# A block-sorted attention with a two-branch network behind it on one core: the first stage's steps join the hand-written list, and the list is laid anew

## The chip, the cores and the metric

One core of a Trainium2 chip. The metric is the device time of one execution in microseconds (us); lower is better. The core's engines are TensorE (PE; its weight loads are shown apart as PEld), VectorE (DVE), ScalarE (ACT), GpSimd (POOL) and SyncE (SP). Each works its own queue of instructions in order, and they meet at semaphores. Here POOL issues all loads, which also turn float32 into bf16; SP issues the transposing DMAs and nearly all stores.

## The reference

```python
# q, k, v: (4, 8, 768, 64); sort_net: (4, 8, 8, 8); block = 96
P = sort_net
for _ in range(5):
    P = P - max(P, -1); P = exp(P)
    P = P / (sum(P, -1) + 1e-9)
    P = P / (sum(P, -2) + 1e-9)
k_sorted = einsum('bhij,bhjcd->bhicd', P, k_blocks)      # the same for v
scores = scale * q_blocks @ k_sorted^T                    # block by block
out = softmax(scores) @ v_sorted
x = out as (3072 tokens, 512)
h1, h2 = x @ w1, x @ w2                                   # w1, w2: 512 x 1024
return max(h1, h2) @ w_out                                # w_out: 1024 x 512
```

## The kernel before

The four batches are worked one after another and overlapped by hand. max(h1, h2) is taken as relu(x (w1 - w2)) + x w2: `d` forms w1 - w2 in place, `T` turns w2 on PE and `c` multiplies it with w_out, so that the second part goes into the output product directly. The output product is done in halves by Strassen's scheme with seven products instead of eight: `P` for two of a half's three token tiles, `U` for the third. The h product of the last batch is done in the same way (`Y`).

Almost all of the work is an order written out by hand: a list of short words, `plan`, that `token` turns into calls one by one. All engines' queues follow from that list: a word appends its instructions to the queue of each engine that it uses, so a word's place is its place in every one of them. A letter at a word's end names the engine that does the conversion out of PSUM or the sum: A for ACT, D for DVE, P for POOL. The words:

- `kb.t`: PE sorts a third of k of batch b, one conversion to kT. `bb.t`: the same for v, into v_sb. `tb.n`: turns a quarter of v (two batches at once) within SBUF, which the sort of v needs. `B`: block diagonals of batches 1 to 3.
- `qb.h`: q turned, by PE and a conversion for b = 0 and 1, by two DMA transposes on SP for b = 2 and 3, which need `pb.0` and `pb.1` (copies that pair heads).
- `sb.u`: scores (8 matrix multiplications) and their exp on ACT. `vb.u`: 8 more, then on DVE a reciprocal `rs` and a multiplication `x`. `xb.t`: x turned into xT, on PE for b = 0 and by an SP transpose for the others.
- `ha`, `hb`, `h`: halves or the whole of an h product, `hb` and `h` with the relu. `X`, `G`, `w`, `Z`: sums for Strassen's scheme (xT, g, weights). `P3.4A`: batch 3, step 4, conversion on ACT.
- `lk`, `lq`, `lf`, `lv`: POOL loads of k, q and v. `y`: POOL waits for xT and qT before it overwrites v_dc.

PSUM has four buffers (`bufs=4`). A word that needs one takes a free one and holds it until its conversion has read it; `P` and `U` hold one over seven steps.

Before the list stands the first stage in plain code: loads of v, k and q of batch 0, five Sinkhorn rounds (`sinkhorn`, a chain of small DVE instructions and one exp on ACT each, with fills on PE), `masks`, the turn of v (`turn_v`, in five parts), `block_diagonals_first` and `sort_k(0, 0)`. The weights' loads follow it, behind two small POOL copies into a tile `seen`, one of which reads `p_bf` (the last Sinkhorn round's result) and the other kT: POOL can't go on to the loads before these exist.

```python
    nc.gpsimd.tensor_copy(out=seen[0:G, 0], in_=p_bf[:, NB - 1, NB - 2 :])
    load_w_columns(w2_sb, moe_w2, 0, 1)
...
    sort_k(0, 0, 640, "A")
    nc.gpsimd.tensor_copy(out=seen[:, 1], in_=kT[0][:, 0:2])
    load_w_columns(w1_sb, moe_w1, 0, 1)
```

Of the kernel before, what the change touches and what calls it, by code (L numbers as in the profile page):

```python
# [1221 lines left out]
```

## Time and profile before

| | |
|---|---|
| three runs | 159.38 (median), 159.37, 160.71 us |
| profiled execution, span | 157.9 us; the page gives no other time for it |
| PE busy | 149.7 us (95%) |
| DVE busy | 127.1 us (81%) |
| ACT busy | 84.4 us (53%) |
| POOL busy | 29.3 us (19%) |
| granted PE clock | full in all 40 slices |

The span runs from the first to the last instruction. "Busy" is time in which an engine has an instruction in work; an engine that issues DMAs or waits isn't busy, except that POOL's own DMA issues are instructions of it. The loads that POOL issues land in this order (issue and landing by the trace, us):

| load | issued | landed | | load | issued | landed |
|---|---|---|---|---|---|---|
| v of batch 0, 3 pieces | 1.24 to 2.40 | 5.50, 7.31, 8.57 | | k1 | 19.63 | 36.05 |
| k0, 3 pieces | 3.47 to 4.56 | 9.81, 11.88, 12.66 | | q1 | 24.43 | 40.04 |
| q0, 4 pieces | 5.08 to 7.59 | 13.64, 14.62, 15.63, 16.57 | | v1, v2, 4 pieces | 25.01 to 27.59 | 42.65 to 47.54 |
| w2 and w1, 4 of 256 KB | 11.40, 13.90, 14.64, 15.96 | 18.65, 19.54, 20.93, 22.23 | | q2 | 31.22 | 51.39 |
| w2 and w1, 2 of 512 KB | 16.69, 17.43 | 24.80, 27.30 | | k2 | 32.67 | 55.27 |
| w_out, 2 of 512 KB | 18.16, 18.89 | 29.89, 32.39 | | k3 | 39.94 | 59.29 |

### The profile page before, as it was taken

What the parts mean: (1) busy time and instruction counts of PE and PEld (TensorE: products, weight loads), DVE (VectorE), ACT (ScalarE), POOL (GpSimd) and SP (SyncE); (2) the same over time, 40 slices, a digit from 0 to 9 for tenths busy, and PEclk for the clock granted to TensorE, in tenths of its full rate; (3) what the DMA queues carried; (4) which work ended last, traced back from release to release, by engine and by line L of the source; (5) the groups of instructions that cost most, each with busy time, mean ns of one, the idle gap of its engine ahead of it and who ended that gap; (6) DMA issues with size and microseconds to landing.
All of it is one profiled execution on the core that took longest, in us unless ns stands there. A gap on an engine that the chain in (4) does not pass through costs nothing.

```text
span 157.9 us, 5185 instructions
## 1 busy us (share of the span) xinstructions
PE 149.7 (95%) x2260; PEld 115.1 (73%) x2264; DVE 127.1 (81%) x274; ACT 84.4 (53%) x111; POOL 29.3 (19%) x57
## 2 busy tenths in 40 slices
PE   6989799999999999999999999999999999999980
PEld 6839577756467788887676898766689886578870
DVE  4879799939969998892899989979878959799340
ACT  3489795656159993459148700793662106692010
POOL 7969997220100000004300000000000000000000
PEclk9999999999999999999999999999999999999999
DMA  2999999999999999795999995750020719000063
GB/s 40 192 204 199 186 202 205 214 214 216 213 203 217 214 145 192 261 132 174 143 220 211 138 147 115 238 215 0 4 50 4 111 42 395 0 4 0 18 254 129
DMA packets 28918, 23.93 MB, mean 152 GB/s; under 512 B 16672, under 2 KB 24608, under 8 KB 28896
## 3 DMA queue, kind: packets, MB, share of 16 engines
q0 software_dynamic: 9280, 13.37, 48.3%
q1 hardware_dynamic: 19200, 9.84, 26.0%
q8 instruction: 17, 0.28, 0.7%
q10 hardware_dynamic: 416, 0.39, 0.7%
q14 instruction: 5, 0.04, 0.1%
HBM read 26.75 MB, written 6.29 MB: 209 GB/s over the span
## 4 chain that ended last, share of the span: by engine, by line
PE 80%; DMA 9%; DVE 6%; issue 1%; POOL 0%; ACT 0%; DVEq 0%; POOLq 0%
PE out_ps L934 33%; PE h_ps L711 20%; DMA q_raw<-in_q_dram 6%; PE wc_ps L691 4%; PE o_ps L609 4%; DMA v_raw<-in_v_dram 3%; PE hb_ps L779 3%; DVE x L626 3%; PE s_ps L581 3%; PE hq_ps L779 2%; PE k_ps L486 2%; PE v_ps L551 2%; PE tw_ps L672 1%; PE tq_ps L453 1%; DVE o L960 1%
## 5 line engine op out<-in xcount | busy, mean ns | idle before, releaser
L711 PE MATMUL h_ps<-xT,w_sb 128*128 128x384 bf16 x192 | 33.9, 326 | 0.1
L597 ACT ACTIVATE e<-s_ps 96x768 bf16<-96x768 f32 x32 | 23.8, 808 | 13.3 <-PE s_ps L581 13.1
L711 PEld LDWEIGHTS <-w_sb 128*128 128x128 bf16 x192 | 17.8, 98 | 10.8
L725 ACT ACTIVATE g<-h_ps 128x768 bf16<-128x768 f32 x20 | 16.0, 812 | 15.1 <-PE h_ps L711 14.9
L626 DVE TENSOR_TENSOR x<-o_ps,rs 96x512 bf16<-96x512 f32 x32 | 22.0, 687 | 1.1
L934 PEld LDWEIGHTS <-g 128*128 128x128 bf16 x192 | 18.3, 98 | 2.3
L934 PEld LDWEIGHTS <-sums_g 128*128 128x128 bf16 x144 | 13.7, 98 | 1.7
L960 DVE TENSOR_TENSOR o<-out_ps,a 128x512 f32<-128x512 f32 (+1 forms) x20 | 11.0, 550 | 3.4 <-PE out_ps L934 2.1
L960 DVE TENSOR_TENSOR o<-out_ps,o 128x512 f32<-128x512 f32 (+1 forms) x16 | 8.8, 555 | 5.6 <-PE out_ps L934 5.5
L934 PE MATMUL out_ps<-wo_sb,g 128*128 128x256 bf16 x96 | 13.1, 273 | 0.0
L609 PEld LDWEIGHTS <-e 96*128 96x128 bf16 x256 | 10.8, 98 | 2.4 <-DVE x L626 0.2
L609 PE MATMUL o_ps<-v_sb,e 96*128 96x65 bf16 x256 | 12.1, 193 | 0.1
L934 PE MATMUL out_ps<-w2T,sums_x 128*128 128x256 bf16 x72 | 11.8, 273 | 0.0
L109 ACT CAST v_sb<-v_ps 96x1024 bf16<-96x1024 f32 x10 | 9.7, 1027 | 0.4 <-PE v_ps L528 0.4
L934 PEld LDWEIGHTS <-sums_x 128*128 128x128 bf16 x96 | 9.0, 98 | 1.2
L581 PE MATMUL s_ps<-qT,kT 64*128 64x96 bf16 x256 | 8.9, 204 | 0.7 <-issue 0.4
L620 DVE RECIPROCAL rs<-o_ps 96x8 f32<-96x8 f32 x32 | 6.3, 197 | 3.4 <-PE o_ps L609 3.2
L581 PEld LDWEIGHTS <-kT 64*128 64x128 bf16 x256 | 6.3, 94 | 3.6 <-issue 2.6
L109 ACT CAST kT<-k_ps 128x1024 bf16<-128x1024 f32 x7 | 7.0, 1013 | 3.4 <-PE k_ps L486 3.4
L969 ACT COPY o<-out_ps 128x512 f32<-128x512 f32 (+1 forms) x7 | 3.5, 503 | 9.7 <-PE out_ps L934 9.7
L111 DVE CAST v_sb<-v_ps 96x1024 bf16<-96x1024 f32 x6 | 7.3, 1216 | 1.2 <-PE v_ps L528 0.8
L779 PEld LDWEIGHTS <-w_sb 128*128 128x128 bf16 x56 | 5.5, 98 | 3.5
(135 smaller groups left out, 272.4 us busy)
## 6 DMA issues: line engine op xcount, KB each, us to landing
out_dram<-o SPq DMA_DIRECT2D x10, 512.0 KB, 3.3
v_raw<-in_v_dram POOLq DMA_DIRECT2D x8, 384.0 KB, 15.5
k_raw<-in_k_dram POOLq DMA_DIRECT2D x3, 768.0 KB, 19.3
w_sb<-in_moe_w_dram POOLq DMA_DIRECT2D x4, 256.0 KB, 6.3
w_sb<-in_moe_w_dram POOLq DMA_DIRECT2D x2, 512.0 KB, 9.0
wo_sb<-in_moe_w_out_dram POOLq DMA_DIRECT2D x2, 512.0 KB, 12.6
v_raw<-in_v_dram POOLq DMA_DIRECT2D x3, 256.0 KB, 5.4
k_raw<-in_k_dram POOLq DMA_DIRECT2D x3, 256.0 KB, 7.9
```

The lines of the kernel that those rows point to most:

```text
L109: nc.scalar.copy(out=out_ap, in_=in_ap)
L111: nc.vector.tensor_copy(out=out_ap, in_=in_ap)
L581: nc.tensor.matmul(ps[:, h2 * 512 + ii * 128 : h2 * 512 + ii * 128 + BLK], kT[b][rows, (hp * 8 + i) * BLK : (hp * 8 + i) * BLK + 128], rhs ...
L597: nc.scalar.activation(out=e_out, in_=src, func=AF.Exp, scale=scale)
L609: nc.tensor.matmul(ps[:, h2 * 512 + ii * 65 : h2 * 512 + (ii + 1) * 65], e[:, (h2 * 4 + ii) * BLK : (h2 * 4 + ii) * BLK + 128], v_sb[:, m0 ...
L626: nc.vector.tensor_tensor(out=x, in0=ov[:, :, :, 0:D], in1=rs.to_broadcast([BLK, 2, 4, D]), op=ALU.mult,)
L691: nc.tensor.matmul(ps[:, 0:512], w2T[:, fb, dmt * 128 : (dmt + 1) * 128], wo_sb[:, fb, :], start=(fb == 0), stop=(fb == NFB - 1),)
L711: nc.tensor.matmul(h_ps[ch, t][:, m * 512 : m * 512 + TCH], w1_sb[:, hp, fb * 128 : (fb + 1) * 128], xT[:, b % 2, ch, hp % 2, hp // 2, :], ...
L725: nc.scalar.activation(out=g, in_=src, func=AF.Relu)
L779: nc.tensor.matmul(ps[:, m * 512 : m * 512 + TCH], w[:, k, c : c + 128], x[:, k], start=new and k == 0, stop=k == 1, skip_group_check=True,)
L934: ins = nc.tensor.matmul(self.ps[:, bank * 512 + p * NW : bank * 512 + (p + 1) * NW], left(self.b, lw, k, ti * 128), right(rw, k), start=n ...
L960: ins = nc.vector.tensor_tensor(out=self.part(ch, half), in0=self.by_tile(self.bank(n)), in1=other, op=ALU.add)
```

## The change

The loads of the first stage are split into single DMAs that have words of their own (`lw`, `lk0.p`, `lq0.p`, `a`), and so have the rest of the first stage (`I` identity, `J` first selections, `S` Sinkhorn rounds, `m` masks, `g` selections, `D0` first block diagonals, `tv` turns of v, `f` fills). All steps are in one list, whose order is new throughout. The two copies into `seen` are gone. w2 comes in four column pieces instead of three. The first sort of k loses its fill of 640 columns, and a fill of the same size (`f4`) stands behind the first Sinkhorn round. The tiles that hold exp's results are taken from a list of free ones instead of in rotation. Some conversions change between ACT and DVE. PE's instructions are the same in number (4530 rows of its queue in both). On POOL, lf1 now comes ahead of k1 and q1, and k3 ahead of k2. On SP, the store of P0's first half and x1.2 now come ahead of q2's transposes.

```diff
@@ -132,7 +132,7 @@
 
     QC = S // 16
 
-    def load_q(b):
+    def load_q(b, part=None):
         if b == 1:
             q_raw[b] = qpool.tile([128, QC * D], BF16, tag="q_raw", name="q_raw", bufs=1)
             nc.gpsimd.dma_start(
@@ -143,10 +143,12 @@
             home = w2_sb.rearrange("p t f -> p (t f)") if b == 2 else v_dc
             t = home[:, 0 : H * R * D].rearrange("p (h x) -> p h x", h=H)
         else:
-            t = qpool.tile([128, H, R * D], BF16, tag="q_raw", name="q_raw", bufs=1)
+            if b not in q_raw:
+                q_raw[b] = qpool.tile([128, H, R * D], BF16, tag="q_raw", name="q_raw", bufs=1)
+            t = q_raw[b]
         src = q[b].rearrange("h (p r) d -> p h (r d)", r=R)
-        for hs in [slice(0, H)] if b else [slice(hp, H, HP) for hp in range(HP)]:
-            nc.gpsimd.dma_start(out=t[:, hs], in_=src[:, hs])
+        hs = slice(0, H) if b else slice(part, H, HP)
+        nc.gpsimd.dma_start(out=t[:, hs], in_=src[:, hs])
         q_raw[b] = t
 
     k_raw = {}
@@ -155,10 +157,11 @@
     v_src = v.rearrange("b h (j c) d -> b (h j) (c d)", j=NB)
     NCH = 3
 
-    def load_k(b):
-        k_raw[b] = kpool.tile([128, HB * D], BF16, tag="k_raw", name="k_raw")
+    def load_k(b, part=0):
+        if part == 0:
+            k_raw[b] = kpool.tile([128, HB * D], BF16, tag="k_raw", name="k_raw")
         n = HB * D // (1 if b else NCH)
-        for ci in range(1 if b else NCH):
+        for ci in [part]:
             nc.gpsimd.dma_start(
                 out=k_raw[b][:, ci * n : (ci + 1) * n],
                 in_=k_src[b, :, ci * n : (ci + 1) * n],
@@ -177,24 +180,20 @@
     w2_sb = big.tile([128, HP, DFF], BF16, tag="w2", name="w2_sb")
     wo_sb = big.tile([128, NFB, DMODEL], BF16, tag="wo", name="wo_sb")
 
-    def load_w(dst, src):
+    def load_w(dst, src, i):
         s = src.rearrange("(t p) f -> p t f", p=128)
         n = s.shape[1] // 2
-        for i in range(2):
-            nc.gpsimd.dma_start(
-                out=dst[:, i * n : (i + 1) * n, :], in_=s[:, i * n : (i + 1) * n, :]
-            )
+        nc.gpsimd.dma_start(
+            out=dst[:, i * n : (i + 1) * n, :], in_=s[:, i * n : (i + 1) * n, :]
+        )
 
     def load_w_columns(dst, src, t0, t1):
         s = src.rearrange("(t p) f -> p t f", p=128)
         c = slice(t0 * DFF // 4, t1 * DFF // 4)
         nc.gpsimd.dma_start(out=dst[:, :, c], in_=s[:, :, c])
 
-    load_v(0, 3)
+    load_v(0, 3, which=0)
     ident = const.tile([128, 128], BF16, tag="ident", name="ident")
-    make_identity(nc, ident)
-    load_k(0)
-    load_q(0)
 
     id64 = const.tile([128, 64], FP32, tag="id64", name="id64")
     maskJ = const.tile([128, 7, NB], FP32, tag="maskJ", name="maskJ")
@@ -219,14 +218,16 @@
         )
 
     one_j = const.tile([G, 8 * 130], BF16, tag="one_j", name="one_j")
-    nc.gpsimd.memset(one_j.bitcast(U32), 0)
-    nc.gpsimd.tensor_copy(
-        out=one_j.rearrange("g (j x) -> g j x", x=130)[:, :, 0:128].rearrange(
-            "g j (h w) -> g j h w", w=16
-        )[:, :, :, 0:2],
-        in_=ident[0:G, 0:8].to_broadcast([G, 8, 2, NB]).transpose([0, 3, 1, 2]),
-    )
-    selections(0)
+
+    def first_selections():
+        nc.gpsimd.memset(one_j.bitcast(U32), 0)
+        nc.gpsimd.tensor_copy(
+            out=one_j.rearrange("g (j x) -> g j x", x=130)[:, :, 0:128].rearrange(
+                "g j (h w) -> g j h w", w=16
+            )[:, :, :, 0:2],
+            in_=ident[0:G, 0:8].to_broadcast([G, 8, 2, NB]).transpose([0, 3, 1, 2]),
+        )
+        selections(0)
 
     def w_difference(t, eng=None):
         n = DFF // 4
@@ -562,7 +563,7 @@
             eng=eng,
         )
 
-    e_tiles, x_tiles, e_next = {}, {}, [0]
+    e_tiles, x_tiles, e_free = {}, {}, list(e_bufs)
 
     def scores(b, u, n=0):
         ih, hp = divmod(u, HP)
@@ -585,8 +586,7 @@
                     start=True,
                     stop=True,
                 )
-        e = e_bufs[e_next[0] % NE]
-        e_next[0] += 1
+        e = e_free.pop(0)
         src = ps[0:BLK].rearrange("p (t f) -> p t f", t=8)[:, :, 0:BLK]
         if b == 1:
             e_out = e[:, 0 : 8 * BLK].rearrange("p (t ch c) -> p t ch c", t=8, ch=2)
@@ -601,6 +601,7 @@
     def values(b, u, n=0):
         ih, hp = divmod(u, HP)
         e = e_tiles.pop((b, u))
+        e_free.append(e)
         m0 = (b % 2) * 64
         ps = ps_f32("o_ps")
         keep_streaming(ps, n)
@@ -1053,40 +1054,20 @@
                         in_=self.both,
                     )
 
-    first, second, both = slice(0, 64), slice(64, 128), slice(0, 128)
+    def spread_masks():
+        for c, n, m in [(2, 2, 0), (4, 3, 1)]:
+            nc.gpsimd.tensor_copy(
+                out=maskJ[:, c : c + n],
+                in_=maskJ[:, m].to_broadcast([128, NB, n]).transpose([0, 2, 1]),
+            )
+
+    first = slice(0, 64)
+    weights = {
+        1: (load_w_columns, w1_sb, moe_w1),
+        2: (load_w_columns, w2_sb, moe_w2),
+        3: (load_w, wo_sb, moe_w_out),
+    }
     keep_streaming(ps_f32("fill_ps"), 92 * 118, most=118)
-    for it in range(5):
-        sinkhorn(it)
-        if it < 3:
-            masks(it)
-        if it == 2:
-            turn_v(first, "A", 0, 18)
-        if it == 3:
-            turn_v(first, "A", 18, 36)
-    for c, n, m in [(2, 2, 0), (4, 3, 1)]:
-        nc.gpsimd.tensor_copy(
-            out=maskJ[:, c : c + n],
-            in_=maskJ[:, m].to_broadcast([128, NB, n]).transpose([0, 2, 1]),
-        )
-    turn_v(first, "A", 36, 56)
-    turn_v(first, "A", 56, 80)
-    block_diagonals_first()
-    seen = const.tile([128, 2, 2], BF16, tag="seen", name="seen")
-    nc.gpsimd.tensor_copy(out=seen[0:G, 0], in_=p_bf[:, NB - 1, NB - 2 :])
-    load_w_columns(w2_sb, moe_w2, 0, 1)
-    selections(1)
-    selections(2)
-    turn_v(first, "D", 80, 96)
-
-    sort_k(0, 0, 640, "A")
-    nc.gpsimd.tensor_copy(out=seen[:, 1], in_=kT[0][:, 0:2])
-    load_w_columns(w1_sb, moe_w1, 0, 1)
-    load_w_columns(w2_sb, moe_w2, 1, 2)
-    selections(3)
-    load_w_columns(w1_sb, moe_w1, 1, 2)
-    load_w_columns(w2_sb, moe_w2, 2, 4)
-    load_w_columns(w1_sb, moe_w1, 2, 4)
-    load_w(wo_sb, moe_w_out)
 
     def token(text):
 
@@ -1095,7 +1076,25 @@
         kind = body.rstrip("0123456789.")
         n = [int(x) for x in body[len(kind) :].split(".")]
         engine = {"P": nc.gpsimd, "D": nc.vector}.get(eng)
-        if kind == "k":
+        if kind == "I":
+            make_identity(nc, ident)
+        elif kind == "J":
+            first_selections()
+        elif kind == "S":
+            sinkhorn(n[0])
+        elif kind == "m":
+            masks(n[0]) if n[0] < 3 else spread_masks()
+        elif kind == "g":
+            selections(n[0])
+        elif kind == "D":
+            block_diagonals_first()
+        elif kind == "tv":
+            turn_v(first, eng, *n)
+        elif kind == "f":
+            keep_streaming(ps_f32("fill_ps"), n[0] * 160, most=320)
+        elif kind == "a":
+            weights[n[0]][0](*weights[n[0]][1:], *n[1:])
+        elif kind == "k":
             sort_k(*n, eng=eng)
         elif kind == "q":
             q_transposes(*n, eng)
@@ -1122,9 +1121,11 @@
         elif kind == "lv":
             load_v(3, half=n[0])
         elif kind == "lk":
-            load_k(n[0])
+            load_k(*n)
         elif kind == "lq":
-            load_q(n[0])
+            load_q(*n)
+        elif kind == "lw":
+            load_v(0, 3, which=n[0])
         elif kind == "w":
             weight_sums(*n, engine)
         elif kind == "c":
@@ -1163,29 +1164,30 @@
     landed = const.tile([128, 4], BF16, tag="landed", name="landed")
     plan = [
         """
-        k0.1D k0.2A b0.2A b0.0D b0.3A q0.0D q0.1D s0.4 b0.1D s0.5 s0.6 s0.7 lk1 v0.4 s0.0 v0.6
-        s0.3 v0.5 d0P s0.1 T1D s0.2 d1P v0.7 x0.2A v0.1 T0A x0.3D ha0.1.0 v0.0 ha0.1.1 v0.2
-        hb0.1.1A lq1 v0.3 lf1 hb0.1.0A x0.0D T3D d3D T2A d2D x0.1A ha0.0.1 ha0.0.0 ha0.1.3
...
+        S0 lw1 f4 I1 lw2 J1 lk0.0 m0 S1 S2 g3 m1 lk0.2 tv0.18A lk0.1 S3 tv36.56A lq0.0 S4 g2 m2 D0
+        tv80.96D tv18.36A tv56.80A k0.0A k0.2D k0.1A lq0.1 b0.2D b0.0A q0.0D b0.1A lq0.2 lq0.3 b0.3D
+        s0.5 q0.1D a2.1.2 a1.0.1 s0.4 s0.1 v0.5 s0.6 v0.4 a2.0.1 s0.7 v0.1 a2.2.3 s0.0 a1.1.2 v0.6
+        x0.2A a1.2.4 v0.7 s0.3 a2.3.4 g1 T1D s0.2 v0.0 d0P a3.0 T0D m3 T2A x0.3D ha0.1.0 d1P d2D
+        x0.0A B0 v0.2 d3D hb0.1.0A ha0.1.2 ha0.1.1 hb0.1.1A hb0.1.2A T3A v0.3 X0.1D ha0.1.3 hb0.1.3A
+        w0.1D G0.0.1D x0.1A G0.1.1D ha0.0.2 ha0.0.1 a3.1 c0A c2A ha0.0.0 w0.3D lf1 lk1 hb0.0.0A
+        X0.2D G0.0.2D hb0.0.1A lq1 lf2 G0.0.3D hb0.0.2D G0.1.3D c1A k1.0D k1.2A k1.1A q1.0D G0.1.2D
+        q1.1A G0.0.4D c3A ha0.0.3 s1.7 w0.2D lf0 w1.1D lf3 X0.3D w1.2D lq2 t1.0D s1.4 w1.3D hb0.0.3A
+        P0.0A s1.6 t1.1D t1.3D s1.5 t1.2D G0.1.4D P0.1D b2.5A b2.1D w0.4D X0.4D b2.0A P0.2A b2.2D
+        p2.0D w1.4D b2.4A s1.1 P0.3D b2.3A b2.7D b2.6A P0.4D s1.2 lk3 v1.4 v1.5 P0.5D v1.6 p2.1D
+        x1.2 q2.0 s1.0 s1.3 P0.6D q2.1 v1.7 U0.0A v1.0 U0.1D v1.2 U0.2A v1.1 v1.3 x1.3 x1.0 x1.1 lk2
+        U0.3D U0.4D k2.2A k2.0D k2.1A U0.5D U0.6D X1.1D s2.7 y1 X1.2D s2.1 s2.4 h1.1.0A h1.1.1A Z1D
+        v2.4 h1.1.3A v2.1 X1.4D G1.1.1D X1.3D h1.0.1D h1.0.0A h1.1.2A G1.1.3D Z2D G1.0.1D lq3
+        G1.1.2D s2.3 s2.0 h1.0.3A k3.0D G1.0.2D G1.1.4D lv0 k3.2A k3.1A h1.0.2D U1.0A U1.1D G1.0.3D
+        lv1 s2.5 G1.0.4D s2.2 s2.6 U1.2D U1.3D U1.4D p3.0A p3.1D v2.3 q3.0 v2.7 U1.5D U1.6D q3.1
+        v2.6 t3.3D P1.0A v2.5 v2.0 P1.1D P1.2A v2.2 s3.0 s3.5 x2.0 t3.2D t3.1D x2.3 P1.3D t3.0D x2.2
+        s3.1 s3.2 s3.3 P1.4D Z3D P1.5D b3.3A s3.4 b3.1D P1.6D b3.2D b3.0A X2.1D h2.1.1D h2.1.3A x2.1
+        Z4D v3.2 v3.4 h2.1.0A v3.1 X2.3D h2.1.2A v3.5 G2.1.1D v3.0 h2.0.1A v3.3 x3.2 h2.0.0A x3.1
+        X2.2D s3.7 s3.6 h2.0.2A G2.0.1D X2.4D G2.0.2D U2.0D v3.7 G2.1.2D G2.0.3D h2.0.3A U2.1D
+        G2.1.4D U2.2D x3.0 G2.0.4D G2.1.3D v3.6 Y3.0.0A U2.3D x3.3 Y3.1.0D U2.4D U2.5D P2.0A U2.6D
+        P2.1D Y3.0.1A P2.2A P2.3D X3.1D X3.2D P2.4D P2.5D Y3.0.2A P2.6D Y3.1.2A X3.3D Y3.0.3A X3.4D
+        Y3.1.1A Y3.1.3A Y3.0.5A Y3.1.5D Y3.0.4A Y3.0.6A Y3.1.4A Y3.1.6D G3.1.1D G3.0.1D G3.0.2D
+        U3.0D P3.0A G3.1.2D G3.0.4D G3.1.3D P3.1D G3.0.3D P3.2A U3.1D U3.2A P3.3A G3.1.4D U3.3A
+        P3.5D P3.4A P3.6D U3.5D U3.4A U3.6D
         """,
     ]
     for part in plan:
```

More of the change, by code (lines that the diff above doesn't have):

```diff
@@ L1165 @@
         """
-        k0.1D k0.2A b0.2A b0.0D b0.3A q0.0D q0.1D s0.4 b0.1D s0.5 s0.6 s0.7 lk1 v0.4 s0.0 v0.6
-        s0.3 v0.5 d0P s0.1 T1D s0.2 d1P v0.7 x0.2A v0.1 T0A x0.3D ha0.1.0 v0.0 ha0.1.1 v0.2
-        hb0.1.1A lq1 v0.3 lf1 hb0.1.0A x0.0D T3D d3D T2A d2D x0.1A ha0.0.1 ha0.0.0 ha0.1.3
-        hb0.1.3A X0.1D X0.2D hb0.0.1A ha0.1.2 hb0.0.0A B0 ha0.0.2 hb0.1.2A w0.3D G0.0.1D w0.1D
-        hb0.0.2A c0A G0.0.2D X0.4D k1.0D k1.1A lf3 lf2 k1.2D X0.3D G0.1.1D c3D G0.1.2D c2D q1.0A
-        q1.1D c1A s1.4 w0.2D w1.1D lf0 G0.1.3D G0.0.3D s1.1 s1.2 ha0.0.3 hb0.0.3A t1.3D t1.2D
@@ L1172 @@
-        w1.2D P0.0A s1.3 t1.1D t1.0D s1.7 s1.6 G0.0.4D w0.4D P0.1D b2.1A G0.1.4D lq2 lk2 b2.3A
-        P0.2A p2.0D w1.3D b2.2D p2.1D b2.4A w1.4D b2.7A P0.3D q2.0 q2.1 b2.5A b2.6D b2.0A P0.4D
-        v1.4 v1.1 P0.5D s1.0 s1.5 v1.7 P0.6D v1.6 v1.5 U0.0A U0.1D k2.0A x1.2 k2.2A v1.0 U0.2A
-        x1.3 v1.2 U0.3D x1.0 v1.3 k2.1A lk3 k3.2D U0.4D s2.7 s2.3 s2.6 U0.5D x1.1 U0.6D s2.2
-        s2.5 s2.0 h1.1.1A v2.7 h1.1.3D v2.3 v2.0 y1 h1.0.1D h1.1.2D h1.1.0A G1.1.1D lq3 v2.6
-        k3.0D G1.0.1D k3.1A G1.1.3D h1.0.0A G1.0.2D h1.0.2A lv0 G1.0.3D s2.4 p3.0A s2.1 X1.1D
@@ L1178 @@
-        P1.0A p3.1D q3.0 X1.2D h1.0.3A G1.0.4D G1.1.2D q3.1 X1.3D Z1D x2.3 X1.4D v2.5 P1.1D lv1
-        U1.0A v2.1 P1.2D v2.4 P1.3D G1.1.4D P1.4D U1.1D v2.2 t3.0D U1.2D U1.3D t3.1D x2.2 x2.1
-        P1.5D U1.4D t3.2D s3.4 s3.5 x2.0 P1.6D s3.7 s3.3 t3.3D U1.5D U1.6D b3.0A b3.1D s3.2
-        h2.1.3A b3.2D Z2D b3.3A h2.1.0A X2.1D X2.2D h2.1.1D G2.1.1D Z4D X2.4D h2.1.2A v3.3
-        G2.0.1D v3.4 h2.0.0A h2.0.1A G2.1.2D h2.0.3A v3.2 x3.1 v3.7 h2.0.2A G2.0.2D v3.5 P2.0A
-        X2.3D s3.1 G2.1.4D s3.0 s3.6 P2.1D U2.0D U2.1D v3.6 G2.1.3D v3.0 G2.0.3D x3.3 U2.2D
@@ L1184 @@
-        P2.2A x3.2 U2.3D v3.1 Z3D P2.3D G2.0.4D x3.0 P2.4D U2.4D U2.5D P2.5D P2.6D U2.6D X3.1D
-        X3.2D X3.3D Y3.1.0A Y3.0.0A Y3.1.1D Y3.1.2A Y3.0.2A X3.4D Y3.0.1D Y3.1.3A Y3.0.3A
-        Y3.0.5A Y3.1.5D Y3.1.4A Y3.0.4A Y3.0.6A Y3.1.6A G3.0.1D G3.0.2D G3.1.1D G3.1.2D P3.0A
-        U3.0D P3.1D P3.2A G3.1.4D G3.0.3D G3.0.4D U3.1D U3.2A G3.1.3D P3.3D P3.5D U3.3A P3.4A
-        P3.6D U3.5D U3.4D U3.6D
+        S0 lw1 f4 I1 lw2 J1 lk0.0 m0 S1 S2 g3 m1 lk0.2 tv0.18A lk0.1 S3 tv36.56A lq0.0 S4 g2 m2 D0
```

## The prediction

> **What bounds the kernel now.** I read the page first (parts 1 and 2), then the busy time by stretch, then the chain of waits in order of time, then the timelines of DVE and of SP's queue.
>
> ```profile
> PE 149.7 (95%) x2260; PEld 115.1 (73%) x2264; DVE 127.1 (81%) x274; ACT 84.4 (53%) x111; POOL 29.3 (19%) x57
> ...
> PEclk9999999999999999999999999999999999999999
> ```
>
> PE is busy for 95% of the span at full granted clock. The change leaves PE's matrix multiplications as they are, in number and size; only their order moves. So it can win no more than the time in which PE is short of work. Where that is:
>
> ```profile
> 10.00:20.00 10.00, 8.78 (x274) 6.96 (x273) 8.10 (x16) 8.64 (x10) 8.49 (x18) 1.00 1.32 193
> 20.00:25.00 5.00, 4.70 (x95) 3.81 (x94) 4.85 (x11) 4.78 (x7) 5.00 (x4) 1.00 1.28 204
> ...
> 60.00:70.00 10.00, 9.93 (x244) 8.52 (x244) 8.78 (x20) 5.09 (x7) 0.00 (x0) 1.00 0.97 204
> ...
> 110.00:120.00 10.00, 10.00 (x120) 7.56 (x118) 7.86 (x19) 5.94 (x8) 0.00 (x0) 1.00 0.10 21
> ```
>
> The columns after the stretch's length are PE, PEld, DVE, ACT and POOL. From 80 us on PE shows no idle time. Before 25 us it does, and "busy" flatters it there, because short matrix multiplications overlap in their records. The chain tells what it waits for:
>
> ```profile
> 7.59 8.98 DMA q_raw<-in_q_dram
> ...
> 18.62 0.43 issue
> ...
> 20.02 0.69 DVE x L626
> 20.70 0.13 DVE rs L620
> 20.83 0.02 issue
> 20.85 0.69 DVE x L626
> ```
>
> The last piece of q lands at 16.57 (7.59 + 8.98). Then the chain is DVE's: value steps (rs and x) follow one another every 0.83 us (20.02 to 20.85), which is 0.06 less for x than its duration, since back-to-back DVE instructions overlap by that much. DVE came late to them:
>
> ```profile
> 17.18 0.96 DVE L111 COPY qT<-tq_ps 128x1536 bf16<-128x1536 bf16 x1 [0.32 <-PE tq_ps L433]
> 18.06 1.21 DVE L111 CAST v_sb<-v_ps 96x1024 bf16<-96x1024 f32 x1
> 19.78 0.20 DVE L620 RECIPROCAL rs<-o_ps 96x8 f32<-96x8 f32 x1 [0.51 <-PE o_ps L609]
> ```
>
> The last conversion of v_sb stands behind both conversions of q on DVE, and no value step can start before it ends at 19.27.
>
> **The change part by part.** A step is named as in the list: b0.1D is sort_v of batch 0, tile 1, converted on DVE.
>
> *First 12.5 us.* The five Sinkhorn rounds keep their order on ACT and DVE; one more mask reduction falls into a later gap (0.25 us, beside PE's nine selections, 11.16 to 11.55). The two 320-column fills (0.15 us each) move from 11.48 to about 7.6; the first sort of k waits for its block diagonal at 11.8 either way. POOL issues the q loads after more copies of selections, so the last of them at about 10.2 and not at 7.59; the ten loads land one behind the other, up to 16.57, so 6 us of queue still cover it. Cost 0. If that cover were gone, it would cost the 2.6 us of the later issue.
>
> *The weights' gates.* The two copies into `seen` go (0.18 us each on POOL), and so does what POOL waited for before them. POOL can issue the first weight load at about 10.9 instead of 11.40 and the following ones 0.75 us apart instead of from 13.90 on. Weights of 256 KB land 1.3 us apart (19.54, 20.93, 22.23), the first two together took 2.97 us after q, so at most 0.4 us of bandwidth is won. One more issue (w2 in four pieces, 0.75 us) lies in that time too.
>
> *12.5 to 31 us.* DVE now does: turn of v to 13.1, k0.2, b0.2, q0.0, b0.3, q0.1. With 1.16 for a conversion of 1024 (1.22 less the overlap) and 0.90 for q that is 13.1 + 1.16 + 1.16 + 0.90 + 1.16 + 0.90 = 18.4. v_sb is ready at 17.5, and half a q is enough for s0.5, so the first value step can start at 18.4 instead of 19.78. From there without a gap: six values (5.0), two turned weights (1.3), x0.3 (0.5) to 25.1; d2 (0.6) must wait for its weights until about 25.6 (1.8 MB behind q; before, the same bytes were in at 26.0 by 22.23 + 3.8), to 26.2; B0 (2.05, by 0.49 + 0.49 + five of 0.22) to 28.2; value, d3, value to 30.5. PE ends hb0.1.3 about 0.6 after d3, h products at 0.16 each: 31.05. Before, the same step ended at 32.02 by the chain, with x0.1 (0.34) done and B0's 0.25 not. That is a lead of 0.9. Bounds: 1.4 (the earlier start kept whole) and 0.3 (weights land no earlier: d2 0.4 later, and a buffer wait of 0.2).
>
> *31 to 51 us.* PE runs through c, h, k1 and q1 on buffered work. k1 and q1 now stand behind a piece of v for batch 2 (384 KB, 1.9 us): q1, at 40.04 before, lands at 41.3 to 42.0, PE needs it at about 42.0. I take 0; at worst 0.6. Then DVE must finish w and the four turns before b2.5: from 45.4 about 5.2 us (three sums of 0.62, 0.5 and three 0.36, four turns at 0.77), to 50.6, where PE comes at 50.1: it waits 0.5. Before, PE began this step's twin at 52.14 with two more scores done (0.45). Lead 52.14 - 50.65 - 0.45 = 1.0, the wait included.
>
> *51 to 72 us.* Before, PE lost 0.20, 0.25 and 0.30 here (at 58.6, 61.1 and 70.3, beyond the normal spacing of its matrix multiplications), each time behind a DVE conversion. In the new list the DVE sum from 50.6 gives p2.1 at 61.8 and k2.0 at 68.8; PE, which runs ahead on three buffers, would come to s2.7 at 69.1 to 69.6. So these 0.75 could go. Bounds: +0.75, and -0.8 if PE can't run ahead, since DVE has 11.2 us of work from b2.5 to p2.1 and PE 8.8. I take +0.7: in the trace PE never waits over 0.3 in this stretch although DVE is as full.
>
> *SP's queue.* These four lines are SP's, in order; the column after the start is the time of the group:
>
> ```profile
> 56.62 3.86 SPq L422 DMA_TRANSPOSE qT<-q_pair  x2
> 61.96 2.25 SPq L974 DMA_DIRECT2D out_dram<-o  x2
> 65.50 5.67 SPq L639 DMA_TRANSPOSE xT<-x  x4
> 72.89 0.37 SPq L1049 DMA_DIRECT2D out_dram<-o  x1
> ```
>
> q2.0 and q2.1 issue for 2.3 and 1.5 us, the four transposes of x for 1.2 to 1.7 each. p2.1, which they wait for, moves from 56.5 to 61.8, and x1.2 and a store come in between: x1.2 to 62.7, q2.0 to 65.0, store 0.4, q2.1 at 65.5, landed 3.8 later, 69.3 (58.99 to 62.8 before). s2.7 wants it at 69.1 to 69.6. Behind q2.1 queue x1.3, x1.0, x1.1, two stores, and so h1.1 and X1. I take 0; the slowest transpose of q in this trace took 5.67 (89.23 to 94.90), which would make 1.7.
>
> *72 us to the end.* PE is full before and the tail is the same chain (the last conversion, U3.6 on DVE, then its store); only U3.4 goes to ACT. Early Y steps hold two more PSUM buffers during P2, and DVE is then some 2.4 us behind PE: between -0.5 and +0.5, taken as 0.
>
> **Sum.** 1.0 + 0.7 = 1.7 off the span: 157.9 - 1.7 = 156.2. The runs' median, 159.38, is 1.5 above the profiled span, and the page gives no other time for that execution, so I add 1.5: 157.7 us.
>
> **The rivals.**
>
> *More is won* (156.4): the first value step's 1.4 us stay whole, the 0.75 too, and the new list also closes what PE lost at 80.0, 82.8 and 102.8 (0.25, 0.39, 0.24): 3.0. For it: ACT takes some 7 us of conversions from DVE. Against: d2's weights, and the turns at 50 us.
>
> *DVE paces 51 to 72* (159.1): the -0.8 above eats the lead, 0.25 is left. For it: 11.2 us against 8.8. Against: three free buffers.
>
> *SP is late* (159.4): q2.1 at 71.2 costs s2.7 1.7 us, all that was won.
>
> *Slower: the weights share the queue with q* (161.3). Ungated, they are issued from 10.9 on while q has 3.7 us (first half) and 5.7 us (all) of transfer left. At half the rate q0.0 is ready at 18.3 instead of 14.6 and its conversion at 20.0 instead of 16.4, so the scores come 3.6 us later and DVE's chain with them: 157.7 + 3.6. It decides from a delay of 3.3 on. For it: gates were the only thing that kept weights out before 11.40. Against: q pieces still landed 0.98, 1.01 and 0.94 apart (14.62, 15.63, 16.57) while four weight loads stood issued behind them (11.40 to 15.96). A late landing of the reordered loads (q1, the pieces of v) is in this rival's chance.
>
> [...]
>
> **How the numbers follow.** Forecast 0.44, its own range 156.6 to 158.8; more won 0.16; DVE paces 0.13; SP late 0.07; slower 0.20. A measurement of this kernel can tell about 1% from no change, 1.6 us. Faster: 0.27 of the forecast's part and 0.16, 0.43. Slower: 0.20 and 0.02 of SP's and the DVE case's far ends, 0.22. Within 1%: 0.35. The range reaches from beyond the larger gain, 155.8, to the slower case, 161.3.
>
> **What would show it.** Right: the first rs at about 18.4, hb0.1.3 ending near 31, b2.5 starting near 50.7 after a wait for v_dc, s2.7 before 70, PE full from 72 on. Wrong: q landing after 17 (the shared queue); PE idle before s2.7 with qT as releaser (SP); idle PE between 52 and 66 behind o and x (DVE); a new idle PE after 72.

## The result, and the profile after

The changed kernel takes 165.51 us (median; 165.28 to 168.17), the kernel before 159.52 in the same rounds: 1.0345 times as long, 95% interval [1.0293, 1.0398]. Run again unchanged it came to 1.0277 [1.0218, 1.0335]. The forecast was 157.7, the range to 161.3. The profiled execution is the longest of the four (168.17, span 166.3), with a mean granted clock of 0.979 against 0.989 to 0.99 in the others, so I read waits and landings from it, and times from the medians.

The page, parts 1, 2 and 3:

```profile
PE 154.1 (93%) x2261; PEld 117.8 (71%) x2264; DVE 123.7 (74%) x268; ACT 89.2 (54%) x117; POOL 29.5 (18%) x56
...
PEclk9999999999999999995599999999999999999999
...
q8 instruction: 17, 0.28, 0.7%
```

PE is busy 4.4 us longer on the same matrix multiplications, and two slices of granted clock stand at half. The stretches that answer to those shown of before, with the one of half clock (PE, PEld, DVE, ACT, POOL, then clock, DMA share, GB/s):

```profile
10.00:20.00 10.00, 8.79 (x253) 6.86 (x252) 8.05 (x17) 7.69 (x8) 5.91 (x9) 1.00 1.31 198
20.00:25.00 5.00, 3.62 (x83) 2.88 (x82) 3.69 (x11) 4.31 (x7) 3.04 (x4) 1.00 1.38 203
60.00:70.00 10.00, 10.00 (x154) 8.66 (x152) 9.59 (x22) 4.42 (x7) 0.00 (x0) 1.00 0.56 88
70.00:75.00 5.00, 3.13 (x109) 2.69 (x108) 3.42 (x7) 2.02 (x2) 0.00 (x0) 1.00 1.30 233
75.00:80.00 5.00, 3.65 (x33) 2.15 (x34) 1.73 (x3) 2.20 (x3) 0.82 (x3) 0.55 0.91 231
```

PE lost 1.1 us more than before in 20 to 25, nothing in 60 to 70, and 3.2 us in 70 to 80, where DVE too works for only half of the time (3.42 and 1.73). The chain of waits, its pieces in order of time, names both places:

```profile
6.41 7.95 DMA k_raw<-in_k_dram
14.36 0.04 issue
14.40 0.69 PE k_ps L487 x32
...
19.65 0.20 PE o_ps L610 x3
19.84 1.06 issue
20.91 0.32 PE o_ps L610 x5
21.23 0.02 issue
21.26 0.21 DVE rs L621
...
70.19 6.03 DMA qT<-q_pair
76.22 0.14 issue
76.36 1.15 PE s_ps L582 x24
```

Where q's last piece set the start before, k's third piece now does (landed 14.36; 12.66 before). In the middle of v0.5's eight matrix multiplications PE then stops for 1.06 us behind nothing that the profile knows ("issue"), and the first rs starts at 21.26, not at 18.4. Later, s2.7 stands from 73.1 to 76.36 behind the transpose q2.1, and the clock is half from 75.5 to 82.3. The waits of PE between 60 and 110 us, all on one tile (total, times, longest), and SP's timeline:

```profile
PE s_ps L582 <- DMA qT<-q_pair: 4.1, 2, 3.2
```

```profile
64.43 0.41 SPq L975 DMA_DIRECT2D out_dram<-o  x1
64.90 1.53 SPq L640 DMA_TRANSPOSE xT<-x  x1
66.53 2.98 SPq L423 DMA_TRANSPOSE qT<-q_pair  x1
69.56 0.58 SPq L975 DMA_DIRECT2D out_dram<-o  x1
70.19 2.01 SPq L423 DMA_TRANSPOSE qT<-q_pair  x1
72.25 4.81 SPq L640 DMA_TRANSPOSE xT<-x  x3
```

p2.1's copy ends at 65.6. On SP x1.2, q2.0 (issuing for 2.98) and a store are still ahead of q2.1, which then needs 6.03 to land. The second of the two waits (0.8) is s3.1 behind q3.1, 30 us later.

### The profile page after: what moved, and what is told of

Same layout as the page of the kernel before. It is cut to its first block, busy times and chain, and to the rows that moved or that the text cites. A ratio compares the mean times of both kernels' runs of the same rounds, so it can differ in the third digit from the quotient of the medians.

```text
span 166.3 us, 5178 instructions
## 1 busy us (share of the span) xinstructions
PE 154.1 (93%) x2261; PEld 117.8 (71%) x2264; DVE 123.7 (74%) x268; ACT 89.2 (54%) x117; POOL 29.5 (18%) x56
## 4 chain that ended last, share of the span: by engine, by line
PE 70%; DMA 12%; DVE 8%; issue 3%; POOL 3%; ACT 2%; SPq 0%; ACTq 0%; POOLq 0%
PE out_ps L935 25%; PE h_ps L712 21%; DMA qT<-q_pair 7%; DMA k_raw<-in_k_dram 5%; DVE x L627 4%; PE wc_ps L692 4%; PE s_ps L582 3%; PE hb_ps L780 3%; PE o_ps L610 2%; PE k_ps L487 2%; PE hq_ps L780 2%; DVE o L961 2%; PE v_ps L508 1%; PE v_ps L552 1%; DVE rs L621 1%
## 5 line engine op out<-in xcount | busy, mean ns | idle before, releaser
L712 PE MATMUL h_ps<-xT,w_sb 128*128 128x384 bf16 x192 | 36.8, 342 | 0.0
L597 ACT ACTIVATE e<-s_ps 96x768 bf16<-96x768 f32 x32 | 24.3, 804 | 8.8 <-PE s_ps L582 8.8
L712 PEld LDWEIGHTS <-w_sb 128*128 128x128 bf16 x192 | 18.2, 101 | 12.5 <-issue 2.4
L582 PE MATMUL s_ps<-qT,kT 64*128 64x96 bf16 x256 | 9.4, 211 | 4.1 <-DMA qT<-q_pair 4.1
L970 ACT COPY o<-out_ps 128x512 f32<-128x512 f32 (+1 forms) x10 | 5.0, 498 | 12.0 <-PE out_ps L935 11.3
L109 ACT CAST v_sb<-v_ps 96x1024 bf16<-96x1024 f32 x9 | 8.9, 1008 | 3.4 <-PE v_ps L529 2.4
L109 ACT CAST kT<-k_ps 128x1024 bf16<-128x1024 f32 x8 | 7.9, 1014 | 4.4 <-PE k_ps L487 4.4
L111 DVE CAST v_sb<-v_ps 96x1024 bf16<-96x1024 f32 x7 | 8.6, 1224 | 0.9 <-PE v_ps L508 0.8
L83 PE MATMUL fill_ps<-fill 128*128 128x118 bf16 (+1 forms) x94 | 8.0, 275 | 1.2 <-DVE fill L74 1.2
```

The lines of the kernel that those rows point to most:

```text
L83: nc.tensor.matmul(ps[:, 0:w], w0, fill[:, 0:w], start=True, stop=True)
L109: nc.scalar.copy(out=out_ap, in_=in_ap)
L111: nc.vector.tensor_copy(out=out_ap, in_=in_ap)
L582: nc.tensor.matmul(ps[:, h2 * 512 + ii * 128 : h2 * 512 + ii * 128 + BLK], kT[b][rows, (hp * 8 + i) * BLK : (hp * 8 + i) * BLK + 128], rhs ...
L597: nc.scalar.activation(out=e_out, in_=src, func=AF.Exp, scale=scale)
L712: nc.tensor.matmul(h_ps[ch, t][:, m * 512 : m * 512 + TCH], w1_sb[:, hp, fb * 128 : (fb + 1) * 128], xT[:, b % 2, ch, hp % 2, hp // 2, :], ...
```

## The experiments

They are called e1 to e17. All are edits of the changed kernel unless another is named; ratios are to the kernel before in the same rounds, with their 95% intervals.

**The late transposes.** Theory: SP's queue costs most of the loss. Rival: the first stage does.

Expected of e1:

> The changed kernel once more, unedited, for a profile like its median run of 165.3 to 165.7 (the profiled execution of it took 168.17). All theories: 165.0 to 166.0. Theory SP: PE waits 2.5 to 3.5 us for the transposed q of batch 2 before s2.7, and the h products after it run at 0.32 us each instead of 0.163. Theory loads: the last piece of q lands 1 us or more after 16.57, and the first value step comes later than 19.78. If the long wait or the slow h products are missing at an unchanged time, theory SP falls.

Measured 1.0277 [1.0218, 1.0335]; four executions from 163.86 (the one in which the clock stayed full) to 170.57. The signs of both theories are in its profile: s2.7 waits 3.3 for q2.1, and q's last piece lands at 18.30.

```diff
- p2.0D ... v1.6 p2.1D x1.2 q2.0 s1.0 s1.3 P0.6D q2.1
+ p2.0D p2.1D q2.0 q2.1 ... v1.6 x1.2 s1.0 s1.3 P0.6D
```

Expected of e2:

> The copy p2.1 and both transposes of q for batch 2 are put right behind p2.0, some 6 us earlier in the list, ahead of x1.2 on SP. Theory SP (the 3.4 us wait and the 2.5 us of half-rate h products behind it make most of the loss): 159.0 to 161.0, no wait before s2.7, h products at 0.163. Rival loads (the loss is made in the first 35 us, and the wait for q would only be replaced by the next wait): 164 or more. Rival DVE (p2.1's 0.5 us earlier makes DVE late for the following conversions): 162 to 164, with PE waiting behind o and x between 55 and 70.

1.0143 [1.0066, 1.0219]; at full clock 160.81, 3.05 less than the 163.86 above. SP's timeline, and PE's at s2.7:

```profile
58.42 3.91 SPq L423 DMA_TRANSPOSE qT<-q_pair  x2
63.34 0.42 SPq L975 DMA_DIRECT2D out_dram<-o  x1
63.81 1.57 SPq L640 DMA_TRANSPOSE xT<-x  x1
```

```profile
71.70 0.38 PE L935 MATMUL out_ps<-w2T,xT 128*128 128x256 bf16 x2
72.01 0.68 PE L582 MATMUL s_ps<-qT,kT 64*128 64x96 bf16 x24
```

The transposes are issued from 58.4 on, and s2.7 follows without a wait. About half of the loss is gone, and half stays.

```diff
- p2.1D x1.2 q2.0 s1.0 s1.3 P0.6D q2.1
+ p2.1D q2.0 q2.1 x1.2 s1.0 s1.3 P0.6D
```

Expected of e3:

> p2.1 stays where it is; only on SP both transposes of q for batch 2 come ahead of x1.2 and of the store of P0's second half. Theory SP by queue order: q lands about 2 us earlier (x1.2's 1.6 and the wait for the store 0.4), the wait before s2.7 shrinks to 1 to 1.5 us and the h products stay at 0.163: 161.0 to 162.5. Theory SP by the late copy: the wait hardly shrinks, 164 to 165.5. If the wait shrinks and the h products still take 0.32 us, the half rate doesn't come from the wait's length.

1.0348 [1.0301, 1.0395]: nothing won. s2.7 waits 1.1 instead of 3.2, but then h1.1.0 waits 1.6 for x1.3's transpose, which lands at 76.17; in the changed kernel it landed at 76.87, hidden by s2.7's wait. This other order on SP isn't enough; its transposes have to start earlier.

In the kernel before, the same part alone:

```diff
- p2.1D b2.4A ... P0.3D q2.0 q2.1 b2.5A ... v1.5 U0.0A U0.1D k2.0A x1.2
+ b2.4A ... P0.3D b2.5A ... v1.5 p2.1D x1.2 q2.0 q2.1 U0.0A U0.1D k2.0A
```

Expected of e6:

> The kernel before, with one part of the change alone: p2.1, x1.2, q2.0, q2.1 in this order behind v1.5, instead of p2.1 at 56 us, q2.0 and q2.1 before b2.5 and x1.2 behind k2.0. Nothing of its first 50 us changes. If SP's queue is the main cause, q2.1 lands at 75 to 78 instead of 62.8, s2.7 (69.6 before) waits 5 to 7 us, and the time is 165 to 169. If the first stage's new order, or the rest of the list, is the main cause, the time stays near 159.7 and at most 1.7 above it (the bound that the prediction gave SP's queue).

1.0244 [1.0135, 1.0353], 3.9 us. PE's waits from 60 to 80 and SP's timeline:

```profile
PE s_ps L581 <- DMA qT<-q_pair: 3.3, 1, 3.3
```

```profile
65.43 1.30 SPq L639 DMA_TRANSPOSE xT<-x  x1
66.83 4.32 SPq L422 DMA_TRANSPOSE qT<-q_pair  x2
```

q2.1 landed at 73.1, earlier than I expected, and the loss is below my 165 to 169; but it is more than twice the bound of 1.7 that the prediction gave, with the first 50 us as they were. Its clock is half from 74.4 to 77.9, too. That SP's queue, with the clock behind its wait, is the largest part is shown from both sides.

**The clock behind the wait.** 24 fill matmuls of 320 columns right before s2.7 (`f48 s2.7`).

Expected of e5:

> The changed kernel, with 24 idle fill matmuls of 320 columns (0.135 us each, 3.2 us in all) put on TensorE right before s2.7, where it waits 3.4 us for q2.1's transpose. They take no data from the wait and change no other engine's work, so q2.1 still lands when it did. If the slow h products behind the wait (0.32 us each for about 3.4 us) are the clock falling after idle time, s2.7 starts as before, the products run at 0.163 us at once, and the kernel gains 1.5 to 2.5 us: 163 to 164. If those products are slow for another reason (their weights, a port, SP's transposes beside them), the time stays at 165.5 within 0.7 and they still take 0.32.

```profile
72.22 3.42 PE L83 MATMUL fill_ps<-fill 128*128 128x320 bf16 x24
75.75 0.69 PE L582 MATMUL s_ps<-qT,kT 64*128 64x96 bf16 x24
76.37 2.77 PE L712 MATMUL h_ps<-xT,w_sb 128*128 128x384 bf16 x16
```

q2.1 still lands at 75.6, but 16 h products now take 2.77 us; with the wait idle, they start 0.32 apart for 16 of them instead of 0.163, 2.5 us more. The granted clock in 75 to 80 us is 1.00 here and 0.55 in the changed kernel, so the slow products are the clock. The time moved little: 1.0328 [1.0255, 1.04], 165.13, not the 163 to 164 that I expected; the other three executions have mean clocks of 0.979, 0.984 and 0.99, so it still fell in them; where, no trace shows.

**The first stage.** First, all loads of v, k and q issued ahead of POOL's copies:

```diff
- lw1 f4 I1 lw2 J1 lk0.0 ... lk0.2 tv0.18A lk0.1 ... lq0.0 ... lq0.1 ... lq0.2 lq0.3
+ lw1 lw2 f4 I1 lk0.0 lk0.2 lk0.1 lq0.0 lq0.1 lq0.2 lq0.3 ...
```

Expected of e4:

> POOL issues all loads of v, k and q of batch 0 before the copies that make the selections, as in the kernel before; the rest is the changed kernel. Theory loads (POOL's copies between the issues let the DMA queue run thin, 116 GB/s in the first 10 us against 136): the last q lands near 16.6 instead of 17.8 and the time falls by about 1: 164.0 to 164.7. Theory SP alone: no change beyond 0.4, since the later wait for q of batch 2 ends when SP's queue ends and not when PE arrives; the time stays at 165.0 to 166.0 unless the copy p2.1 comes earlier too.

The last piece of q landed at 16.47 instead of 17.8, as expected, but the time was 1.0449 [1.0385, 1.0514], worse. The stop in v0.5 was 1.33 us (counted, here and below, from the start of one matrix multiplication to the start of the next, less their usual spacing; the 1.06 in the chain above is 1.23 so) and the clock then half from 21.1 to 27.9; all four executions had a mean clock of 0.979 or less.

Then three waits at once, `lf1` behind `lq1` and `p3.0A p3.1D q3.0 q3.1` behind `U1.1D` on top of the early transposes:

Expected of e7:

> The changed kernel without its three late transposes: p2.1, q2.0, q2.1 right behind p2.0 (as in the run of these alone, 162.9), and two further edits: lf1's load behind lq1's instead of ahead of lk1 (takes 0.6 us of waiting from q1.1 at 44.5), and p3.0, p3.1, q3.0, q3.1 moved ahead behind U1.1 (takes 0.95 from s3.1 at 98.6). If these waits are added to the end one by one: 161.3 (160.8 to 162.0), and above the kernel before by what the first 27 us lost (1.0 to 1.7). If DVE's order paces 84 to 100, or the copies of p3 push U1's evictions back, the gain is 0.6 or less: 162.3 or more.

1.0101 [1.0065, 1.0137]. The wait before s3.1 is gone, one of 0.3 behind DVE is new at 90.9, and the profile has a stop of 1.42 at 18.7 and less clock behind it (the page's digits 8 and 7 in the two slices from 20 to 28 us). The idle time at 46 us only shrank (0.52 to 0.39), and I had taken it wrongly for a wait for q1. PE's timeline in the changed kernel:

```profile
45.24 0.76 PE L454 MATMUL tq_ps<-ident,q_raw 64*64 64x64 bf16 x37
46.52 1.11 PE L454 MATMUL tq_ps<-ident,q_raw 64*64 64x64 bf16 x59 [0.52 <-issue]
```

q1 landed at 43.63 in one DMA, and PE has done 37 of the turn's 96 matrix multiplications when it stops, behind nothing that the profile knows, as in v0.5.

With the early loads and six fills of 512 columns (`F4` ahead of s0.6, s0.7, s0.0, v0.7, s0.3, s0.2):

Expected of e8:

> The run with the three waits taken away, with GpSimd issuing all loads of v, k and q ahead of its own copies (last q piece at 16.5 instead of 17.8), and six idle fill matmuls of 512 columns (0.216 us each) on TensorE where it waits in 20 to 25 us, ahead of s0.6, s0.7, s0.0, v0.7, s0.3 and s0.2. The run of the loads alone had the half clock at 21 to 28. If it came from TensorE's sparse work there, the fills keep the full clock and the first value step's start, 1.0 us earlier, reaches the end: 0.5 to 1.5 us under the run without fills. If the half clock comes from the stop at 18.4 (1.3 us, in which no releaser is shown), the fills come too late, the half clock stays in 21 to 28 and the time is the same as without, or up to 1.5 above.

1.0103 [1.0011, 1.0194], and repeated below 1.0077 [1.0038, 1.0116]: the stop is there (1.32), the clock stays full. Against e7 nothing is won that the intervals would show.

**What the stop is.** The queue `q8 instruction` has 17 packets of 16 KB in the changed kernel (the line above) and 18 in e5, which adds instructions of PE alone, so I took these packets for blocks of PE's instructions. In the DMA records the second of them starts to move at 17.4 in e8 and at 18.5 in the changed kernel, and PE goes on at 19.71 and 20.91. In all profiles with such a stop, it ends 2.2 to 2.5 us after that start. If it is a wait for that block, it must move when the number of instructions ahead of it changes.

```diff
- keep_streaming(ps_f32("fill_ps"), 92 * 118, most=118)
+ keep_streaming(ps_f32("fill_ps"), 92 * 118)
```

Expected of e9:

> The changed kernel with the early transposes (162.9; 160.8 where the clock stayed full) and its first fill as 22 matmuls of 512 columns in place of 92 of 118: the same columns, but about 140 fewer TensorE instructions (a load and a matmul each) before the first step. If the stop of 1.0 to 1.8 us in the middle of v0.5, shown as issue, is TensorE waiting for its next block of instructions, it moves some 140 instructions down the list, to 21 to 24 us, where TensorE has spare time: v0.5 ends without a stop, the first value step's reciprocal starts at 19.0 instead of 20.2, and the time falls by 0.5 to 1.2 to about 162. If the stop belongs to v0.5 itself (its tile, the exponential), it stays at 18.4 and the time is 162.9 within 0.7.

1.0202 [1.0174, 1.0231], slower. The stop moved, from v0.5 to a sort of v at 16.9, so it isn't v0.5's own; but it moved to an earlier step, not a later one, and grew to 1.57. The first block now started to move at 16.1 instead of 10.6, and the stop ended 2.4 us after that. Another stop came at 49.8 (1.2).

The traces settle the place. PE's waits show at least 19 stops of over 0.35 us behind nothing that the profile knows, in 16 profiles, that of the kernel before included. Count the instructions of PE's queue in each kernel (matrix multiplications, weight loads and a few for its sequencer): all 19 lie in the step whose instructions have 449 (2 stops), 705 (14) or 1473 (3) ahead of one of them, and these numbers are multiples of 256 apart. Where the timeline shows at which instruction PE goes on, it is that one: in v0.5 of the changed kernel, e8 and e16, behind three of eight matrix multiplications, 705 stand ahead, and inside q1's turn, behind 37, 1473. e9's two stops are those at 449 and 1473. What PE waits for there no record names; that it is the next block is my inference from the 2.2 to 2.5 us. Why e9's first block started to move so late, no run shows.

With all mends at once (e8, these fills, `v1.4 v1.5` behind `P0.5D`, p3 behind `lv1`):

Expected of e10:

> All the mends at once: the run with fills and early loads (161.1), its first fill as 22 wide matmuls, v1.4 and v1.5 behind P0.5 (0.5 us of waiting for b2.7's copy at 59.5), and p3's copies behind G1.0.3 instead of ahead of it (0.4 at 88.6). If the waits are additive: 161.1 less 1.0 for the stop and 0.9 for these two, 159.2, level with the kernel before within 1 per cent. If the stop only moves, or VectorE paces the first value steps, 160.2 or more.

1.0494 [1.0445, 1.0544], the worst of all. PE's waits from 15 to 75 us:

```profile
PE v_ps L508 <- issue: 2.2, 1, 2.2
PE wc_ps L692 <- issue: 2.2, 1, 2.2
PE s_ps L582 <- DVE x L627: 1.4, 2, 0.9
```

PE stopped twice for 2.2 us behind nothing that the profile knows, and moving v1.4 put s behind DVE. 34 more instructions in e8 (`most=100`):

Expected of e14:

> The same run without gates, its first fill as 109 matmuls of 100 columns instead of 92 of 118 (the same columns, 34 TensorE instructions more ahead of the first step). If the stop falls where a block of instructions ends, it comes about 34 instructions earlier in the list, in q0.1 or s0.5, and its length changes with how fast TensorE runs there: 160.5 to 162. If the stop is bound to v0.5, nothing changes: 161.1 within 0.6 and a stop of 1.3 at 18.4.

1.0155 [1.0095, 1.0215]: the stop moved to s0.4 and s0.1 (again 705 instructions stand ahead of it) and took 2.08 us, with the clock at 0.60 in 21 to 24.

**The gates.** Both copies into `seen` put back, ahead of the first weight load and of the second (the words `e0` and `e1` of this list stand for the two copies):

```diff
- s0.5 q0.1D a2.1.2 a1.0.1 s0.4
+ s0.5 q0.1D e0 a2.1.2 e1 a1.0.1 s0.4
```

Expected of e11:

> The changed kernel with the two gates put back: GpSimd copies from p_bf ahead of the first weight load, and from kT ahead of the second. The prediction gave them at most 0.4 us. If that holds, the last q piece lands within 0.3 us of where it does without them (17.8 and 18.3 in two runs) and the time is that of the changed kernel, 165.5 within 0.8. If loading the weights without a gate is what slows the first stage, q lands 0.5 to 1.5 earlier and the time falls by as much.

1.033 [1.0283, 1.0377]: no difference, by the time. But its profile shows no stop in v0.5. So, with the transposes early:

Expected of e13:

> The changed kernel with the early transposes (162.9, stop of 0.96 us in v0.5 at 18.6) and both gates put back ahead of the first weight loads. If the gates take the stop away, v0.5 runs through, the first value step's reciprocal starts at 19.2 instead of 20.2, and the time is 161.5 to 162.2. If the missing stop was one execution's luck, it is there again, and the time is 162.9 within 0.7.

1.0111 [1.0057, 1.0165] against 1.0143 without; the stop is still there (0.92). And in e8:

Expected of e12:

> The run with early transposes, early loads and fills (161.1, stop of 1.3 us at 18.4), with both gates put back. If the gates take the stop away: 159.8 to 160.3, level with the kernel before. If not: 161.1 within 0.6.

1.0008 [0.9988, 1.0028] over ten executions, level with the kernel before. Since these intervals touch those without gates, the pair was repeated in the same rounds, and the gates were taken out of the kernel before (the two `tensor_copy` lines into `seen` deleted, nothing else):

Expected of e16:

> The run with early transposes, early loads and fills once more, without gates: 161.1 in four runs. If the gates matter, 160.8 to 161.5 again, and over its twin with gates by 0.8 to 1.3. If not, the two come out within 0.4 of each other.

Expected of e17:

> The same with both gates, once more: 160.0 in ten runs. 159.8 to 160.3 if the gates matter; level with its twin without them if not.

Expected of e15:

> The kernel before without its two gates, nothing else. If the gates keep the first stage's stop short and so the clock full, some of its executions lose 1 to 2 us more and the median rises by 0.5 to 1.5, to 160.3 to 161.3. If they do nothing by themselves (the order of GpSimd's other work already holds the weights back), it stays within 0.3 of 159.8.

Without gates 1.0077 [1.0038, 1.0116], with them 1.0012 [0.9983, 1.0041]; the kernel before without its gates 1.0087 [1.0052, 1.0122] of itself, 1.4 us. The intervals of e16 and e17 still touch at their ends, but compared directly the two are 1.2 us apart, with a 95% interval of 0.5 to 1.9 (means of 161.11 over 8 executions and 159.92 over 12). Of five pairs, three agree (e8 and e12, e16 and e17, the kernel before and e15), and the one in the kernel before excludes zero. e2 and e13 can't be told apart, with the stop in both; the changed kernel and e11 show nothing, with q2.1's wait behind it. PE's timeline in v0.5 without gates (first fence) and with them:

```profile
18.33 0.27 PE L610 MATMUL o_ps<-v_sb,e 96*128 96x65 bf16 x3
19.67 0.31 PE L610 MATMUL o_ps<-v_sb,e 96*128 96x65 bf16 x5 [1.08 <-issue]
```

```profile
18.63 0.61 PE L610 MATMUL o_ps<-v_sb,e 96*128 96x65 bf16 x8
```

And the stretch of the stop by engine and bandwidth, again without and with:

```profile
18.00:21.00 3.00, 1.92 (x44) 1.17 (x38) 1.81 (x4) 1.98 (x3) 0.19 (x1) 1.00 1.45 194
```

```profile
18.00:21.00 3.00, 2.97 (x65) 1.88 (x60) 2.76 (x6) 2.77 (x5) 1.33 (x4) 1.00 1.30 166
```

The second block's start and PE's stop behind it in the profiles of all lists with the original number of instructions ahead, us (* half clock follows within the first 31 us):

| with gates | block, stop | without | block, stop |
|---|---|---|---|
| before | 16.6, 0.61 | e15 | 17.5, 1.01 |
| e6 | 16.7, 0.60 | e2, e3 | 17.4, 0.96 and 18.2, 1.15 |
| e11 | 16.5, none | e5 | 18.2, 0.79 |
| e12 | 16.6, 0.65 | e8, e16 (fills behind) | 17.4, 1.32 and 1.24 |
| e17 | 16.6, 0.20 | e4, e7 | 17.3, 1.33* and 17.7, 1.42* |
| e13 | 17.4, 0.92 | changed kernel, again (e1) | 18.5, 1.23 and 19.4, 1.78* |

The three lists with another number of instructions had stops of 1.57*, 2.08* and 2.34*. With gates the block starts to move 0.7 us or more earlier than in any list without, in five of six. That the weights' transfers delay it is an inference from the lower rate (166 against 194 GB/s); what decides when a block starts to move no run shows.

## Why the prediction was wrong, by its steps

- *SP's queue*, taken as 0 with 1.7 as the worst: the step that failed most. The mechanism was written down (p2.1, x1.2, q2.0, a store, q2.1) and so was its sign, "PE idle before s2.7 with qT as releaser". The term was mis-sized. From the end of p2.1's copy to q2.1's landing I allowed 7.5 us (61.8 to 69.3); it took 10.6 (65.65 to 76.22): q2.0 issued for 2.98 and not 2.3, the store for 0.58 and not 0.4, and the landing took 6.03 and not 3.8. PE went from the same point to s2.7 in 7.5 us (to 73.1), as forecast (7.3 to 7.8). I took the 5.67 in the trace of before for the worst case only. POOL's loads don't explain it: the last of them landed at 89.33, 0.1 us after that transpose was issued. In the new order none was under way between 60.1 and 79.8, and q2.1 took 6.03 all the same; in e1, e3 and e5 it took 6.04, 6.61 and 6.09.
- *72 us to the end*, taken as 0: wrong, since I took the granted clock as given. The idle time before s2.7 went over into 6.8 us of half clock in the profile, 2.8 us of PE (24 products of scores in 1.15 instead of 0.69, 16 of h in 5.15 instead of 2.77); by their mean clock of 0.99 the other three executions had half as much. And s3.1 waited 0.8 for q3.1, a transpose that I didn't follow.
- *The weights' gates*, at most 0.4 won: wrong in sign. Taking them out costs 1.4 us in the kernel before, with q's landing hardly moved (16.88 against 16.57). The rival "the weights share the queue" named the place but not the way: pieces of q still land 0.95 to 1.04 apart with weights issued behind them, so that mechanism is refuted. My sign for it, q after 17, came true (17.78) for another reason: without gates but with the loads issued first, q was in at 16.47. What is lost stands in PE's stop and its clock: in the profile of e15 the stop is 1.01 instead of 0.61, and ten of its twelve executions have a mean clock of 0.988 or less, against three of 26 with the gates.
- *First 12.5 us*, cost 0 since "6 us of queue still cover it": wrong. In 8 to 10 us the loads moved 130 GB/s against 212 before; k's third piece came 1.7 late and q's last 1.2. With the loads issued first it was 202 GB/s and q in time. By itself that mend gained nothing: the clock fell behind the stop, and s2.7 still waited 3.3.
- *12.5 to 31 us*, lead 0.9: wrong. hb0.1.3 ended at 34.35 instead of 31.05. k's landing is some 1.7 of it, and another 1.2 is the stop, which the sum had no row for, though the chain of before showed "18.62 0.43 issue". The 1.7 is this execution's: in e1, e2, e3, e5 and e7, with the same loads, k's third piece came 0.7 to 2.0 late.
- *31 to 51 us*, q1 taken as 0: right by luck. q1 landed at 43.63, not 41.3 to 42.0, but PE, late by then, came to it only at 45.24. What PE lost there, 0.5, was the stop with 1473 instructions ahead, which the sum had no row for. b2.5 began at 54.42 instead of 50.65, and 3.3 of these 3.8 are hb0.1.3's.
- *51 to 72 us*, +0.7: right. PE's waits of 0.20, 0.25 and 0.30 are gone (one of 0.19 is left), and from b2.5 to s2.7 PE took 18.7 us, as forecast (50.65 to 69.1 or 69.6). DVE doesn't pace; with p2.1 early (e2) one wait of 0.4 behind its conversion to v_sb comes back, and s2.7 runs on without a gap.

How the loss of 4.4 to 5.5 us adds up, by ratios: the transposes with the clock behind them 2 to 3 (1.0277 to 1.0345 down to 1.0143; 3.05 between two single executions at full clock), the gates 1.0 to 1.5. The rest, down to 1.001, came with q3's earlier transposes, the load order and the fills, whose shares the intervals don't separate. With all of these mended the new order is level with the old; no version beat it. Against the forecast, the profiled span of 166.3 misses 156.2 by 10.1: 3.8 by b2.5, nothing more up to s2.7, 3.2 of waiting there, 2.8 of half clock and 0.8 before s3.1, less 1.2 by which the last store landed sooner after its issue (1.87 instead of 3.04); 0.7 stays open.

The half-clock stretches were 3.5 us long in e6 (74.4 to 77.9) and 6.8 in the changed kernel (75.48 to 82.31) and in e4 (21.1 to 27.9). A stop's length alone doesn't tell whether one follows: behind stops of 1.33 (e4) to 2.34 us (e10) the clock fell, behind those of 1.32 in e8 and 1.24 in e16 it didn't. What decides it, no run shows.

## What to carry to other kernels

A moved step that ends in a DMA is priced from the moment its data are ready to the landing, with every entry of that queue ahead of it at the slow end of its durations, not the median. A wait on PE can cost more than itself: here the clock fell behind a stop of 1.33 us (e4) and behind a wait of 3.2 (the changed kernel), and stayed full with 24 fills in that wait (e5) and with six fills behind a stop of 1.32 (e8). And a gate that delays loads can pay for itself, by 1.4 us in the kernel before (e15): take it out alone before dropping it.
